# A third SBUF buffer for a unit's q and M in a fused attention and feed-forward kernel

## The chip, the cores and the metric

The kernel runs on one core of one Trainium2 chip. The metric is the device time of one execution in microseconds. The engines are named as the profile names them: PE (matrix products) with PEld (its weight loads), DVE (vector), ACT (scalar), POOL and SP. All transfers of this kernel are issued from SP's queue. Each engine works through its own queue in order, and waits on semaphores of the others.

## The reference, cut

Four sequences of 576 tokens with 8 heads of 64 go through causal attention and a retrieval from a memory matrix M; a gate mixes both, and a feed-forward layer with squared ReLU follows.

```python
scores = scale * np.matmul(q, k.transpose(0, 1, 3, 2))          # causal, softmax -> a
local = np.matmul(a, v)
q_p = np.where(q > 0, q, np.exp(q) - 1.0) + 1.0                  # phi
mem_out = einsum('bhsd,bhde->bhse', q_p, M_prev) / (einsum('bhsd,bhd->bhs', q_p, z_prev)[..., None] + 1e-06)
x = g * mem_out + (1 - g) * local                                # g = sigmoid(beta), per head
out = np.maximum(x @ w_in, 0.0) ** 2 @ w_out                     # 512 -> 2048 -> 512
```

## The kernel before

**Units.** Attention is cut into 24 units, called u0 to u23 here. A unit is one sequence, one pair of heads (their 2 x 64 rows fill the 128 partitions) and a set of query tiles of 128 tokens. The first two sequences have two kinds of units, four with tiles 1 and 2 and then four with tiles 3 and 4; the last two sequences have four units each with all four tiles. (The first 64 tokens of each sequence are done apart at the start.)

**Loads of a unit.** `loads` issues three tiles: `kd` (k, one buffer, `KB = 1`), `qm` (M, z and q, `QB` buffers, line 348; units of tiles 3 and 4 take two transfers, one for M and z and one for q) and `vv` (v, two buffers, `VVB = 2`). They are requested by `after()` in line 464, when the products with M of the unit before have been written down; the first unit's at the start.

**A unit's work.** From u6 on q and k are split into a high and a low part: ACT writes `qh` (line 371), DVE `ql` (372), ACT `kh` (377), POOL or DVE `kl` (378). u0 to u5 use q and k as loaded. ACT takes exp of q (388), and phi is formed, from u6 on in place in `qm` (393, 394), before that in `pe` (399, 400). v is scaled by its largest element (`vx`, `vt`, `vy`) and split into `vs` (425, 427). PE multiplies phi with M (`pm`, line 445, whose PSUM tag `av` has two buffers that it shares with `vt` and `acc`), and that is the last read of a unit's `qm`. Then come the scores (`sp`, line 479, one PSUM buffer), the row minimum and mask on DVE (500), exp on ACT (520), the split of the weights into `a` (558, 560), their transpose by DMA (`aT`, 564), the product with v (`acc`, 585 to 590), and the sum into `memx` (600), which is written to DRAM (611). `qh`, `ql`, `kh` and `kl` have one buffer each.

**Feed-forward.** The tokens are taken in nine blocks. `moe(n)` runs 8 steps: 24 products `up` with the first weight (747 to 749), ReLU and square on ACT (753, 754), a split into `gh` and `gl` (756 to 759), and 12 products with the second weight into `oacc` (737 to 739). In its seventh step it fetches the tokens of the next block (`xn`, 632), transposes them on PE (635, 637) into a PSUM buffer of the tag `up`, and splits them on ACT (640) and DVE (641). The last two blocks run together (`moe_pair`, lines 666 to 721). The weights are loaded and split in stages through about the first 90 us.

**Order.** The program is written down unit by unit; `ORD` merges the first units with the weights and with block 0, the rest of attention follows, and then the other blocks. A planner (`schedule_with_timeline_sim=True`) then fixes, while the program is built, the order of every engine's queue: what is written down first has priority, and what is written later fills the time that is free. So blocks 1 and following run between the attention units. A load into a tile with buffers waits for the last reader of the tile that had the buffer before: with `QB = 2` the `qm` of unit n waits for `pm` of unit n-2.

Of the kernel before, what the change touches and what calls it, by code (L numbers as in the profile page):

```python
# [43 lines left out]
PXT = 'av'  # L44
PXE = 'aa'
PHI = 1
QB = 2
VVB = 2
ZW = D + 1
MW = 576  # L50
# [42 lines left out]
def fused_kernel(ctx: ExitStack, tc: tile.TileContext, t0_d, kk_d, qv_d, beta, w_in, w_out, out):  # L93
# [247 lines left out]
    def loads(b, p, tiles):  # L341
        qa, qb = QT[tiles[0]][0], sum(QT[tiles[-1]])
        kd = at.tile([P, S], F32, tag="kd", name="kd", bufs=KB)
        nc.sync.dma_start(kd[:, :qb], kk_d[b, p, :, :qb])
        qm = at.tile([P, 2 * ZW + SQ], F32, tag="qm", name="qm", bufs=QB)
        qa, qb = qa - D + 2 * ZW, qb - D + 2 * ZW
# [552 lines left out]
```

## Time and profile before

| | us |
|---|---|
| time, median of 3 runs (lowest to highest) | 578.53 (578.21 to 580.98) |
| the profiled execution | 578.71 |
| its span | 576.9 |
| PE busy (share of the span) | 550.8 (95%) |
| PEld busy | 478.6 (83%) |
| DVE busy | 414.0 (72%) |
| ACT busy | 349.6 (61%) |
| POOL busy | 63.7 (11%) |

The span is the time between the first and the last event that the profile shows; 1.8 us of the profiled execution lie outside of it. Busy times of PE and PEld overlap. PEclk is the clock that TensorE was granted, as a share of its full 2.4 GHz. "Waits" rows say which instruction an engine's queue was held at, and what ended the hold.

### The profile page before, as it was taken

To read this page: it belongs to the slowest core of one execution; us is meant where nothing else is said; L and a number is where in the kernel's file an instruction comes from. 1 tells how busy PE (TensorE), PEld (TensorE's weight loads), DVE (VectorE), ACT (ScalarE), POOL (GpSimd) and SP (SyncE) were. 2 spreads that over 40 slices of the span, in tenths; PEclk is the share of its full clock that TensorE was granted. 3 is DMA by queue.
4 is the path that set the end of the run, shared out by engine and by line. 5 is a ranking of instruction groups with operands and counts; after the bars stand their busy time and mean duration, and the time that the engine had idled before them with its cause. 6 is when DMAs were issued, how large, how long until landed. Compare 5 with 4: busy or idle time off the path is not lost.

```text
span 576.9 us, 11597 instructions
## 1 busy us (share of the span) xinstructions
PE 550.8 (95%) x4259; PEld 478.6 (83%) x4259; DVE 414.0 (72%) x1323; ACT 349.6 (61%) x792; POOL 63.7 (11%) x45
## 2 busy tenths in 40 slices
PE   5489998898999999999999999999999999999997
PEld 5378886787888888898988988889889898888885
DVE  6989989897989888989695988969787523212121
ACT  4589976767868767877567675665756222212213
POOL 3749560012010000000000000000000000000000
PEclk9999999799999999999999999999999999999999
DMA  8857654875665466676456736675244610000001
GB/s 310 341 192 286 228 168 111 174 162 136 138 150 159 109 183 151 149 185 168 110 108 124 149 78 163 115 189 143 56 84 83 128 37 1 36 2 0 1 0 73
DMA packets 124856, 74.71 MB, mean 129 GB/s; under 512 B 97152, under 2 KB 110464, under 8 KB 124800
## 3 DMA queue, kind: packets, MB, share of 16 engines
q1 hardware_dynamic: 124800, 73.98, 49.7%
q8 instruction: 33, 0.54, 0.4%
q14 instruction: 23, 0.19, 0.1%
HBM read 41.59 MB, written 8.78 MB: 87 GB/s over the span
## 4 chain that ended last, share of the span: by engine, by line
PE 63%; DVE 12%; ACT 10%; DMA 9%; issue 3%; POOL 1%; SPq 1%; ACTq 0%; DVEq 0%; POOLq 0%
PE oacc L677 8%; PE up L747 6%; PE up L749 6%; PE up L748 6%; PE oacc L737 6%; PE oacc L739 6%; PE oacc L738 6%; PE sp L479 5%; DMA vv<-in_qv_dram 4%; ACT e L520 3%; PE up L692 3%; PE up L691 3%; PE up L693 3%; PE acc L590 2%; PE pm L445 2%
## 5 line engine op out<-in xcount | busy, mean ns | idle before, releaser
L747 PE MATMUL up<-xh,w 128*128 128x256 f32 x448 | 129.5, 289 | 0.0
L748 PE MATMUL up<-xl,w 128*128 128x256 f32 x448 | 128.9, 288 | 0.0
L749 PE MATMUL up<-xh,w 128*128 128x256 f32 x448 | 128.4, 287 | 0.0
L520 ACT ACTIVATE e<-e,mx 128x320 f32<-128x320 f32 (+3 forms) x128 | 77.6, 608 | 50.1 <-DVE memx L600 34.1
L737 PE MATMUL oacc<-w,gh 128*128 128x512 f32 x224 | 89.9, 402 | 0.0
L747 PEld LDWEIGHTS up<-xh,w 128*128 128x128 f32 x448 | 86.0, 192 | 2.9 <-issue 0.6
L738 PE MATMUL oacc<-w,gh 128*128 128x512 f32 x224 | 88.4, 395 | 0.0
L748 PEld LDWEIGHTS up<-xl,w 128*128 128x128 f32 x448 | 86.1, 192 | 2.2
L739 PE MATMUL oacc<-w,gl 128*128 128x512 f32 x224 | 86.4, 397 | 0.4 <-DVE gl L759 0.4
L749 PEld LDWEIGHTS up<-xh,w 128*128 128x128 f32 x448 | 86.1, 192 | 0.7
L560 DVE SCALAR_TENSOR_TENSOR a<-e,a 128x128 f16<-128x128 f32 x116 | 64.1, 566 | 31.1 <-ACT a L558 30.1
L558 ACT ACTIVATE a<-e 128x128 f16<-128x128 f32 x116 | 55.0, 524 | 10.9 <-DMA aT<-a 9.9
L753 ACT ACTIVATE r<-up 128x512 f32<-128x512 f32 x56 | 32.7, 584 | 43.2 <-PE up L749 29.0
L702 DVE CAST gh<-r 128x512 fp32r<-128x512 f32 x15 | 6.4, 427 | 62.4 <-ACT r L701 62.4
L739 PEld LDWEIGHTS oacc<-w,gl 128*128 128x128 f32 x224 | 41.5, 188 | 9.0 <-DVE gl L759 0.9
L738 PEld LDWEIGHTS oacc<-w,gh 128*128 128x128 f32 x224 | 42.3, 189 | 6.6
L500 DVE CUSTOM_DVE_ANT_0 e<-sp,mask 128x320 f32<-128x320 f32 (+3 forms) x128 | 47.0, 417 | 0.9 <-PE sp L479 0.7
L737 PEld LDWEIGHTS oacc<-w,gh 128*128 128x128 f32 x224 | 42.3, 189 | 6.4
L700 ACT ACTIVATE r<-up 128x512 f32<-128x512 f32 x16 | 9.6, 597 | 60.8 <-PE up L693 60.8
L759 DVE TENSOR_TENSOR gl<-r,gh 128x512 fp32r<-128x512 f32 x56 | 38.9, 695 | 2.6 <-ACT gh L756 1.8
L677 PE MATMUL oacc<-w,gh 128*128 128x512 f32 x120 | 36.8, 389 | 0.0
L590 PE MATMUL acc<-vs,aT 128*128 128x128 f16 x302 | 36.7, 220 | 0.0
(153 smaller groups left out, 1160.2 us busy)
## 6 DMA issues: line engine op xcount, KB each, us to landing
raw<-in_w_in_dram SPq DMA_DIRECT2D x11, 512.0 KB, 7.2
vv<-in_qv_dram SPq DMA_DIRECT2D x16, 320.0 KB, 3.3
raw<-in_w_out_dram SPq DMA_DIRECT2D x9, 512.0 KB, 6.6
kd<-in_kk_dram SPq DMA_DIRECT2D x16, 288.0 KB, 3.1
out_dram<-o SPq DMA_DIRECT2D x16, 256.0 KB, 2.1
xd<-memx SPq DMA_DIRECT2D x31, 128.0 KB, 1.9
xn<-xd SPq DMA_DIRECT2D x14, 256.0 KB, 2.9
qm<-in_qv_dram SPq DMA_DIRECT2D x8, 321.0 KB, 2.9
```

The source lines that it names most:

```text
L500: nc.vector.tensor_tensor_reduce(out=e[:, h, ka:kb], in0=sps[:, h, cs], in1=mask[:, 448 - q0 + ka : 448 - q0 + kb], scale=-0.125, scalar=3 ...
L520: ex = nc.scalar.activation(e[:n, h, :ke], e[:n, h, :ke], AF.Exp, bias=bs, scale=-1.0, accum_out=sm[:n, h : h + 1])
L558: nc.scalar.mul(av[:, :, o0 : o0 + w], x, SC)
L560: nc.vector.scalar_tensor_tensor(out=av[:, :, o0 + w : o0 + 2 * w], in0=x, scalar=SC, in1=av[:, :, o0 : o0 + w], op0=ALU.mult, op1=ALU.sub ...
L590: nc.tensor.matmul(o2, aT[:, h * nb + c, :n], vs[:, h, c], start=False, stop=c == i)
L677: mms.append(nc.tensor.matmul(acc[t], g[:, ts], w_out_op(f, part), start=s0, stop=s1))
L737: nc.tensor.matmul(acc[t], gh[:, u, ts], w_out_op(f, 0), start=f == 0, stop=False)
L738: nc.tensor.matmul(acc[t], gh[:, u, ts], w_out_op(f, 1), start=False, stop=False)
L739: nc.tensor.matmul(acc[t], gl[:, u, ts], w_out_op(f, 0), start=False, stop=f == NF - 1)
L747: nc.tensor.matmul(up[:, u, :], w_in_op(f, k, 0), xh[:, k, :], start=k == 0, stop=False)
L748: nc.tensor.matmul(up[:, u, :], w_in_op(f, k, 0), xl[:, k, :], start=False, stop=False)
L749: nc.tensor.matmul(up[:, u, :], w_in_op(f, k, 1), xh[:, k, :], start=False, stop=k == NK - 1)
```

## The change

The pool of the tile `qm` gets three buffers in place of two. One constant is changed, and no instruction is added or removed in the code; a buffer is 642 floats of each partition (2 x 65 for M and z, 512 for q).

```diff
-QB = 2
+QB = 3
 ...
         qm = at.tile([P, 2 * ZW + SQ], F32, tag="qm", name="qm", bufs=QB)
```

With three buffers the load of unit n waits for `pm` of unit n-3.

## Rows read from the trace of the kernel before

**Rows 1.** The page, its first part: busy time, share and instructions by engine.

```profile
PE 550.8 (95%) x4259; PEld 478.6 (83%) x4259; DVE 414.0 (72%) x1323; ACT 349.6 (61%) x792; POOL 63.7 (11%) x45
```

**Rows 2.** Windows: length, PE, PEld, DVE, ACT, POOL busy (instructions), PEclk, DMA share, GB/s.

```profile
17.00:34.00 17.00, 10.19 (x232) 9.49 (x232) 15.14 (x29) 9.90 (x17) 13.20 (x7) 1.00 0.58 230
92.00:110.00 18.00, 14.26 (x82) 10.92 (x82) 16.55 (x63) 8.66 (x19) 0.94 (x2) 0.81 0.84 175
102.00:109.00 7.00, 5.98 (x26) 4.83 (x27) 5.86 (x24) 4.89 (x10) 0.84 (x1) 0.52 0.71 167
110.00:140.00 30.00, 28.86 (x243) 23.84 (x243) 25.76 (x84) 23.55 (x52) 2.97 (x2) 1.00 0.71 165
140.00:170.00 30.00, 28.97 (x250) 25.11 (x248) 25.26 (x93) 21.51 (x59) 3.51 (x3) 1.00 0.63 142
170.00:230.00 60.00, 59.65 (x480) 52.58 (x477) 52.79 (x190) 45.17 (x107) 1.02 (x1) 1.00 0.56 144
230.00:440.00 210.00, 210.00 (x1739) 185.32 (x1738) 173.99 (x603) 140.46 (x325) 0.00 (x0) 1.00 0.59 131
465.00:490.00 25.00, 25.00 (x154) 22.30 (x154) 7.11 (x14) 7.65 (x15) 0.00 (x0) 1.00 0.01 1
```

**Rows 3.** Timeline of PE, 229.7 to 231.3 and 480 to 484: start, duration, line.

```profile
229.80 0.28 PE L747 MATMUL up<-xh,w 128*128 128x256 f32 x1
229.92 0.28 PE L748 MATMUL up<-xl,w 128*128 128x256 f32 x1
...
480.86 0.28 PE L747 MATMUL up<-xh,w 128*128 128x256 f32 x1
480.98 0.28 PE L748 MATMUL up<-xl,w 128*128 128x256 f32 x1
```

**Rows 4.** Waits of SP's queue: total us, times, longest us.

```profile
SPq L351 <- DVE vs L427: 16.6, 14, 3.0
SPq L348 <- PE pm L445: 15.0, 8, 5.0
```

**Rows 5.** The load of qm (line 348): who waited for it, us and times.

```profile
  ACT pe L388: 5.7, 3
  ACT qh L371: 4.2, 4
```

**Rows 6.** Timeline, 238.5 to 250 us: SP's loads and the steps that take them.

```profile
240.27 0.71 PE L445 MATMUL pm<-qm 128*128 128x130 f32 x4
241.02 0.33 SPq L348 DMA_DIRECT2D qm<-in_qv_dram  x1
242.28 0.33 SPq L351 DMA_DIRECT2D vv<-in_qv_dram  x1
244.46 0.61 ACT L371 CAST qh<-qm 128x512 fp32r<-128x512 f32 x1
246.64 0.68 DVE L372 TENSOR_TENSOR ql<-qm,qh 128x512 fp32r<-128x512 f32 x1
248.83 0.42 PE L479 MATMUL sp<-kh,qh 64*128 64x320 f32 x2
```

**Rows 7.** Timeline, 97.7 to 112 us; in brackets the idle time before and what ended it.

```profile
98.05 0.90 SPq L348 DMA_DIRECT2D qm<-in_qv_dram  x2
...
99.53 0.38 SPq L344 DMA_DIRECT2D kd<-in_kk_dram  x1
...
100.36 0.30 PE L637 MATMUL px<-identr,memx 128*128 128x128 f32 x1
...
101.99 0.42 ACT L388 ACTIVATE pe<-qm 128x256 f32<-128x256 f32 x1 [2.81 <-DMA qm<-in_qv_dram]
102.31 0.57 ACT L640 CAST xh<-px 128x512 fp32r<-128x512 f32 x1
...
103.86 2.18 PE L479 MATMUL sp<-kd,qm 64*128 64x448 f32 x8 [1.02 <-DMA kd<-in_kk_dram]
...
106.78 0.41 PE L747 MATMUL up<-xh,w 128*128 128x256 f32 x1
...
106.99 0.41 PE L748 MATMUL up<-xl,w 128*128 128x256 f32 x1
```

## The prediction

> **What bounds the kernel now.** I first read the shares: PE is busy for 95% of the span, DVE for 72% [rows 1]. A share over the whole span hides stages, so the second view is the table of windows [rows 2]. The reader should see three regimes there. Up to 34 us PE is idle much of the time (10.19 of 17.00 us busy from 17 to 34), because the weights and the first tokens are being prepared. From 92 to 230 us PE has small gaps: 18.00 - 14.26 = 3.74 us between 92 and 110, 1.14 to 140, 1.03 to 170 and 0.35 to 230. From 230 to 440 us, where the last nine units or so of attention run between blocks of the feed-forward, PE shows no idle time at all (210.00 of 210.00), nor in the stretch without attention from 465 to 490.
>
> Ends of matmuls are modelled, so a busy PE could hide bubbles. The third view is therefore the distance between starts [rows 3]: 256-column products start 0.12 us apart both beside attention (229.80, 229.92) and alone (480.86, 480.98). Beside attention PE runs at the pace that it has alone, so from 230 us on the time is set by the amount of PE work, and the change takes none away.
>
> The clock is the other thing to see. Between 102 and 109 us the granted clock is 0.52 of full speed, that is nearly all of it at 1.2 GHz [rows 2]; the 256-column products start 0.21 us apart there (106.78, 106.99) [rows 7] in place of 0.12. What PE did before is the gap of 3.74 us. At full clock the 5.98 us of PE work in that stretch would need at least 5.98 x 0.52 = 3.1 us, so the slow clock costs up to 2.9 us. Gap and clock together are 6.6 us, the largest loss after the start.
>
> **What the change removes: the wait of the qm load.** SP's queue stood 15.0 us, in 8 waits, at line 348 until a `pm` product had been done [rows 4]. One case is seen in full [rows 6]: `pm` of u14 starts at 240.27 and takes 0.71; the load of u16 goes out at 241.02, at once; ACT writes `qh` of u16 3.4 us after that (244.46), `ql` comes at 246.64 and the scores at 248.83. So a load that has its buffer one unit earlier would let `qh` come up to 3.4 us sooner in a unit. But that wait stands on the path of attention, not on that of PE: while u16 waits, PE runs products of the feed-forward. What ACT itself lost by waiting for `qm` is 5.7 + 4.2 = 9.9 us in 7 waits [rows 5], on an engine that is busy for 61% [rows 1].
>
> Step by step, by stretches, against the profiled execution of 578.71 us (576.9 span and 1.8 outside):
>
> 0 to 92 us. The load of u2 has a buffer of its own and no wait; it can go out behind the first weight loads, in the stretch from 17 to 34 us, where the DMA engines are busy for 0.58 of the time [rows 2]. Each later load takes the place in SP's queue where the load of the unit before stood, so, if the planner keeps that order, no queue gets longer. I take 0. The bounds are a gain of 0, since the units up to u4 start long after their `qm` has landed (ACT's waits for it number only 7, and the first that I can place is at 101.99), and a loss of 0.9 us, the issue time of two transfers of this kind [rows 7], if they stand ahead of a load that the start waits for.
>
> 92 to 110 us. Here `qm` is on PE's path for once [rows 7]. The load of u5 goes out at 98.05. ACT's queue stands at line 388 for it until 101.99 (2.81 us idle). Behind that instruction is the copy `xh` of block 1's tokens (102.31), though its transpose on PE started at 100.36 and took 0.30. The `up` products of block 0 wait for the PSUM buffer that this copy frees. With three buffers u5 only waits for `pm` of u2, a whole unit earlier, so `xh` can start at about 100.7, 1.6 us sooner. The next to be late is the scores of u5 on PE, which are queued ahead of the `up` products and waited for `kd` until 103.86; `kd` has one buffer and went out at 99.53, behind the two `qm` transfers (0.90 us of SP's time). So the gain is between 0 (if `kd` stays where it is) and 1.6 us, and I take 0.9, what `kd` gains if the two transfers are not ahead of it. The ends for the range are wider: all of 6.6 us, if the gap closes enough that the clock is not lost, and a loss of 0.9, if the loads of u6 stand ahead of `kd` with nothing to show for it.
>
> 110 to 230 us. PE's idle time is 1.14 + 1.03 + 0.35 = 2.52 us in all, and DVE is busy for 25.76 of 30, 25.26 of 30 and 52.79 of 60 us (86%, 84%, 88%) [rows 2]. Earlier `qh` and `ql` can close part of these gaps, none of which is put down to `qm` directly. Bounds: 0 and 2.52; I take 0.6, about a quarter, since the load of `vv`, which waits for `vs` of the unit before last (16.6 us in 14 waits, [rows 4]), stays and becomes the wait that holds SP: in the case of [rows 6] it is 1.26 us behind the `qm` load.
>
> 230 us to the end. 0: no idle time to take [rows 2], the same work, the same pace [rows 3].
>
> The sum is 0.9 + 0.6 = 1.5 us, so 577.2 us against the profiled execution. That execution was 0.18 us above the median of the runs, so I say 577.0 us.
>
> **The rivals.**
>
> The gap closes. Between 92 and 110 us the queues are planned anew, PE gets `up` products or scores in time, and the clock stays at 2.4 GHz. Gain 6.6 us there and about 1 us behind it: 571.1 us. For it speaks that a wait for `qm` is in the chain of this gap; against it that `kd`, the last units' `memx` and DVE (16.55 of 18.00 us busy) are in it too.
>
> PE has hidden room beside attention, and a shorter attention gives it back. Weight loads are busy for 185.32 of 210.00 us, 0.882, from 230 to 440, against 22.30 of 25.00, 0.892, without attention [rows 2]; the difference is 1.1% of 210 us, or 2.3 us, which with the sum above gives 574.9 us. Against it are the equal distances of [rows 3]. [...]
>
> A second gap, on the other side. Because q is there earlier, the planner puts the splits and exponentials of the next unit ahead on ACT and DVE. In the stretch from 110 to 230 us DVE has only 12 to 16% free. Where it gets none, `gl` of the feed-forward comes late, PE runs out of products as it did at 100 us, and the clock falls. The place is a unit's start in that stretch; it decides once DVE is busy for as much as between 92 and 110 us (92%). The price is that of the gap that is there, 3.74 + 2.9 = 6.6 us: 585.1 us by the median, less if part of the sum is gained: 583.6.
>
> Nothing moves. The load is earlier, but `vv` (two buffers) and `kd` (one) take the place of the wait, and PE's gaps are the same: 578.5 us. For it speaks that `vv` follows by 1.26 us in [rows 6].
>
> **How the numbers follow.** The forecast (1 to 2 us saved) gets 0.31, nothing moves 0.14, the gap closes 0.25, hidden room 0.06, a second gap 0.24. The likeliest gives 577.0. A measurement of this kernel can tell about 0.5%, 2.9 us, from no change: faster means below 575.6, slower above 581.4. The first two cases lie within; hidden room and the closed gap lie below; the second gap above, with a few hundredths of it within, where the new gap costs no clock. That makes 0.31 faster, 0.47 the same, 0.22 slower. The range has to take in the closed gap with all of the idle time behind it, 578.5 - 6.6 - 2.5 = 569.4, and the second gap, up to 585.1; leaving the outermost part of both out, it is 570.0 to 584.0. The likeliest case alone would be 574.9 to 578.5.
>
> **What would show it.** Right: the loads of `qm` wait for no `pm`, or hardly, and ACT's 9.9 us of waits for them are gone; SP stands longer at `vv`; PE stays without idle time from 230 us on; the stretch around 100 us keeps a gap of 2 to 4 us and a slow clock. Wrong: a change of more than 1 us behind 230 us, which would mean that PE's amount of work isn't the limit there; a gap around 100 us that is gone, or a new one with a clock of 0.5 elsewhere. The start would be wrong if PE's busy time before 34 us shifts by more than the 0.9 us that I bounded.

## The result and the profile after

| | before | after |
|---|---|---|
| time, median of 8 runs each (lowest to highest), us | 578.86 (576.50 to 581.23) | 582.62 (581.85 to 584.55) |
| ratio, 95% interval | | 1.0051 (1.0027 to 1.0074) |
| the profiled execution, us | 578.71 | 582.10 |
| its span, us | 576.9 | 580.3 |

The third buffer made the kernel about 0.5% slower; the forecast was 577.0 us, 0.26% faster. PE's amount of work did not change. The first part of the page of after answers to [rows 1]:

```profile
PE 550.7 (95%) x4259; PEld 479.7 (83%) x4259; DVE 412.6 (71%) x1323; ACT 349.0 (60%) x792; POOL 62.8 (11%) x45
```

Its windows, with the columns of [rows 2]:

```profile
92.00:110.00 18.00, 13.34 (x75) 10.26 (x75) 16.28 (x62) 8.56 (x18) 1.06 (x2) 0.82 0.73 166
110.00:140.00 30.00, 30.00 (x253) 25.21 (x253) 26.48 (x88) 25.06 (x56) 3.14 (x2) 1.00 0.79 179
140.00:170.00 30.00, 30.00 (x264) 26.46 (x262) 27.45 (x103) 23.38 (x64) 4.18 (x4) 1.00 0.64 148
170.00:230.00 60.00, 59.09 (x470) 52.16 (x469) 52.00 (x183) 44.71 (x104) 0.00 (x0) 1.00 0.63 148
...
290.00:305.00 15.00, 12.57 (x119) 11.38 (x119) 12.21 (x43) 8.39 (x23) 0.00 (x0) 0.89 0.66 117
...
400.00:440.00 40.00, 38.95 (x309) 34.17 (x307) 32.13 (x118) 23.37 (x53) 0.00 (x0) 1.00 0.32 64
```

Against [rows 2], PE's idle time between 110 and 230 us fell from 2.52 to 0.91 us in this execution: a gain of 1.6. Between 92 and 110 us it rose from 3.74 to 4.66. And where PE had no idle time at all, 2.43 us appeared between 290 and 305 us, with a granted clock of 0.89 of full speed, and 1.05 us between 400 and 440. Those two new gaps are more than the gain. They are there too in a second profiled execution of the same program (e8 below: 2.26 and 1.03 us); the slow clock beside the first is not (1.00 there).

What PE waited for near 298 us is in the timeline of SP, PE and ACT (start, duration, line; in brackets the idle time before and what ended it).

```profile
291.71 6.11 SPq L564 DMA_TRANSPOSE aT<-a  x2
...
297.35 0.45 PE L635 MATMUL px<-identr,xn 128*128 128x128 f32 x4
300.23 0.23 PE L585 MATMUL acc<-vs,aT 128*128 128x128 f16 x1 [2.43 <-DMA aT<-a]
...
300.27 0.83 ACT L558 ACTIVATE a<-e 128x128 f16<-128x128 f32 x2 [1.47 <-DMA aT<-a]
301.01 0.57 ACT L640 CAST xh<-px 128x512 fp32r<-128x512 f32 x1
```

The waits of after (total us, times, longest us):

```profile
SPq L351 <- DVE vs L427: 27.0, 14, 4.5
SPq L348 <- PE pm L445: 22.0, 9, 5.3
...
ACT a L558 <- DMA aT<-a: 18.2, 16, 2.6
PE acc L585 <- DMA aT<-a: 3.5, 2, 2.4
PE sp L479 <- DMA kd<-in_kk_dram: 2.9, 1, 2.9
ACT qh L371 <- DMA qm<-in_qv_dram: 1.9, 1, 1.9
```

The view of line 564 of after tells how long its transposes took from issue to landing; in the kernel before that line reads 2.5/3.9/5.7.

```profile
DMA to landing us min/median/max: 2.8/4.1/6.2
```

The transposes of the weights `a` by DMA (line 564) came late. PE's queue stood at the product `acc` that needs one; ACT stood at the copy into `a` whose buffer the transpose was to free, and `xh` of the feed-forward's tokens was queued behind it, so PE could not fill the gap with `up` either. The loads of `qm`, on which the change was argued, are no longer an issue for ACT (1.9 us here and 1.4 at line 388, against 9.9 in [rows 5]). But they still wait for `pm` on SP, longer than in [rows 4] (22.0 us against 15.0).

### The profile page after: what moved, and what is told of

The parts are those of the page before. It is cut to its first block, busy times and chain, and to the rows that moved or that the text cites. A ratio compares the mean times of both kernels' runs of the same rounds, so it can differ in the third digit from the quotient of the medians.

```text
span 580.3 us, 11585 instructions
## 1 busy us (share of the span) xinstructions
PE 550.7 (95%) x4259; PEld 479.7 (83%) x4259; DVE 412.6 (71%) x1323; ACT 349.0 (60%) x792; POOL 62.8 (11%) x45
## 4 chain that ended last, share of the span: by engine, by line
PE 77%; DVE 9%; DMA 7%; POOL 3%; issue 3%; ACT 1%; SPq 1%; DVEq 0%; POOLq 0%; ACTq 0%
PE up L747 8%; PE up L748 8%; PE up L749 8%; PE oacc L677 8%; PE oacc L737 7%; PE oacc L739 7%; PE oacc L738 7%; PE sp L479 7%; PE acc L590 3%; PE up L693 3%; PE up L692 3%; PE pm L445 3%; PE up L691 2%; DMA aT<-a 2%; POOL raw L180 2%
```

## The experiments

All were timed against the kernel before on the same chip; ratios are to it, with 95% intervals. Executions of the kernel before itself spread between 576.4 and 584.8 us in these batches, so one of them alone says little below 1%.

### The order or the waits?

The planner makes a new order of all queues for three buffers. Four runs took order and waits apart. **e1_old_order** keeps every queue in the order of the plan for two buffers and has three; only the waits of the `qm` loads differ.

```diff
+    nc, arrays = build(2, None)          # QB = 2: its queues give the order
+    nc, arrays = build(3, queues(nc))    # QB = 3 in that order
+    for n, m in zip(seq, seq[1:]):
+        tc.add_manual_dep(ins[m], n, AFTER, reason="order of the other plan")
```

> Three buffers, but every engine's queue keeps the order that the planner made for two buffers; only the waits of the qm loads for pm are gone. Theory A (the loss comes from the new order of the queues, and PE did not wait for qm): PE's idle time from 92 us on stays within 1 us of that of the kernel before, no gap near 300 us, 577 to 579 us. Theory B (the earlier loads themselves disturb the transposes or other transfers): transposes land later than the 3.9 us median of before, and the time is 581 to 584 us, as after.

**e2_swap** is the changed kernel with two transposes of the gap at 298 us exchanged on SP, so that the one that PE waits for is issued first.

```diff
+    seq.remove("I-3278")
+    seq.insert(seq.index("I-3317"), "I-3278")
```

> The changed kernel with the order of its queues kept, but for one pair: the two transposes that SP issued at 291.7 and 294.5 us change places, so that the one for which PE stood until 300.2 us goes first. Theory A' (the loss is this one gap, an order of two transposes): the gap of 2.4 us and its slow clock go, the time falls by 2 to 4 us to 579 to 580. Theory B (three buffers cost in general, and the gap only shows where): the gap moves, 582 to 583 us.

**e3_two_written** (two buffers) and **e4_three_written** (three) hold the transposes in the order in which they are written down and let the planner place the rest.

```diff
-                nc.sync.dma_start_transpose(out=aT[:, :, :n], in_=a[:n])
+                turn(tc, nc.sync.dma_start_transpose(out=aT[:, :, :n], in_=a[:n]))   # behind the last one
```

> A control with two buffers: the planner is only told to keep the transposes in the order in which they are written down, which gives new orders on PE, DVE, ACT and SP. Theory A (what the change moved is mainly the luck of a new plan): the time differs from before by 1 to 4 us, in a direction that I can't foresee, 575 to 583 us, with gaps of PE at other places. Theory B (a plan's details matter little, three buffers cost): 578.3 to 579.5 us.

> Three buffers with a third plan: the transposes are kept in the order in which they are written down. Theory A: no loss that belongs to three buffers, 576 to 581 us, and the gap near 298 us is gone, since its two transposes were out of the written order. Theory B: 582 to 584 us as after.

| | median, us | ratio |
|---|---|---|
| e1_old_order | 586.95 | 1.0100 (1.0072 to 1.0129) |
| e2_swap | 581.91 | 1.0025 (1.0001 to 1.0049) |
| e3_two_written | 580.82 | 0.9988 (0.9963 to 1.0013) |
| e4_three_written | 579.09 | 0.9962 (0.9937 to 0.9987) |

e1 was the surprise. With the queues of the kernel before and waits only taken away, it should have been no slower than 577 to 579 us; it was slower than the changed kernel. So the new order of the queues could not be the whole cause, and something else had come with the third buffer. e2 has a smaller gap (13.55 of 15.00 us busy from 290 to 305 us, against 12.57), but its gain on the changed kernel can't be told from none. e3 shows that the written order of the transposes alone is worth nothing that can be told; with three buffers (e4) the kernel is 0.4% faster than before.

### The early loads or the place of the tiles?

Two things were left in e1: the `qm` loads go out earlier, and the third buffer (642 floats, which take 2592 bytes as allocated) moves every tile that lies behind `qm` in SBUF. **e5_same_waits** keeps the order and gives the loads back the waits that they have with two buffers, so only the places differ. **e6_first_free** frees the loads of u2 to u7 alone, **e7_last_free** those of u8 to u23; **e8_after_again** is the changed kernel, held to its own order in the way in which e5 to e7 are held to the old one.

```diff
+    for load, readers in TIED.items():   # e5: all units, e6: u8 to u23, e7: u2 to u7
+        for n in readers:                # what the load waits for with two buffers
+            tc.add_manual_dep(ins[load], n, DependencyInfo(DependencyClass.Sync, DependencyReason.DATA), ...)
```

> Three buffers, but every queue in the order of the plan for two buffers, and every load of qm waits for the same instructions as with two buffers (pm of the unit before last). Against the kernel before, only the places of tiles in SBUF differ. Theory C (it is the early loads that cost: the transfers that now go out earlier meet the transposes and stores and delay these): ratio 0.9975 to 1.0025. Theory D (the place of the tiles costs, not the waits): 1.007 to 1.013, as with the old order and free loads.

> As the run before in this batch, but the loads of u2 to u7 are free to go one unit earlier (they wait for pm of the third unit before, or nothing). Theory C: the old order with free loads was 1.6 us behind the kernel before at 112 us and 3.3 us at 165 us of the span, so 1.003 to 1.006. Theory D: 1.007 to 1.013.

> The complement: the loads of u8 to u23 are free, those of u2 to u7 wait as with two buffers. Theory C: the old order with free loads lost another 5 us behind 200 us, so 1.004 to 1.008. Theory D: 1.007 to 1.013. If C is right the two parts together give the 1.0% of the old order with free loads.

> The changed kernel itself (three buffers, its own order, its own waits), on this chip, as the measure for the other three. Both theories: 1.003 to 1.007, as in its own comparison. A ratio of 1.000 or below would mean that its loss belongs to single executions and not to the order.

| | median, us | ratio |
|---|---|---|
| e5_same_waits | 587.16 | 1.0081 (1.0048 to 1.0114) |
| e6_first_free | 588.72 | 1.0119 (1.0082 to 1.0157) |
| e7_last_free | 586.20 | 1.0083 (1.0054 to 1.0112) |
| e8_after_again | 583.41 | 1.0040 (1.0013 to 1.0067) |

Theory C falls, theory D stands: with the same instructions, the same order and the same waits, the kernel is 0.8% slower once its tiles lie elsewhere, and which loads are free makes no difference that can be told. The way of holding an order costs nothing that can be told either: e8 is as slow as the changed kernel itself (1.0040 and 1.0051).

### Which places?

The kernel before has nearly all tiles on a grid of 64 bytes, and a third buffer moves them 32 bytes off it (2592 = 40 x 64 + 32). **e9_same_waits_aligned** is e5 with the tile of k 32 bytes larger, which restores that grid. **e10_two_shifted** is the kernel before, two buffers, with that same enlargement, which breaks it. **e11_after_aligned** and **e12_three_written_aligned** put the changed kernel and e4 on the grid by a wider `qm`.

```diff
-        kd = at.tile([P, S], F32, tag="kd", name="kd", bufs=KB)
+        kd = at.tile([P, S + 8], F32, tag="kd", name="kd", bufs=KB)                 # e9, e10
...
-        qm = at.tile([P, 2 * ZW + SQ], F32, tag="qm", name="qm", bufs=QB)
+        qm = at.tile([P, 2 * ZW + SQ + 14], F32, tag="qm", name="qm", bufs=QB)      # e11, e12
```

> The run with three buffers in the old order and with the old waits, but the tile of k is 32 bytes larger, so that every tile behind qm begins at a multiple of 64 bytes of its partition again (the third buffer had moved them all by 2592 bytes, 32 more than a multiple of 64). Theory D1 (a begin off the 64-byte grid costs): 0.9975 to 1.0025. Theory D2 (another effect of the place, or of the third buffer, whatever the grid): 1.005 to 1.011, as without the 32 bytes.

> The kernel before with two buffers and nothing else changed than the tile of k, 32 bytes larger: all tiles behind it begin 32 bytes off the 64-byte grid. Order and waits are those of the kernel before. Theory D1: 1.005 to 1.011, without any third buffer; transposes land at 4.1 us in the median in place of 3.9. Theory D2: 0.9975 to 1.0025.

> The changed kernel with the tile of qm 14 floats wider, so that its buffers are 2624 bytes apart and all tiles begin on the 64-byte grid; order and waits are those of the changed kernel. Theory D1: it gives back the 0.8% of the place, from 1.004 to 0.994 to 0.999, which is what the prediction said of the waits. Theory D2: 1.001 to 1.007.

> Three buffers, transposes in the written order (0.9962 before), and the tile of qm 14 floats wider as in the run before. Theory D1: another 0.4 to 0.8% faster, 0.988 to 0.993. Theory D2: 0.994 to 0.999.

| | median, us | ratio |
|---|---|---|
| e9_same_waits_aligned | 586.42 | 1.0109 (1.0078 to 1.0141) |
| e10_two_shifted | 586.48 | 1.0100 (1.0070 to 1.0130) |
| e11_after_aligned | 582.70 | 1.0043 (1.0020 to 1.0066) |
| e12_three_written_aligned | 579.64 | 0.9986 (0.9963 to 1.0008) |

Neither theory fits: e9, e11 and e12 came out as D2 has it, e10 as D1. The 64-byte grid is not it, and yet the place counts: e10 has 32 bytes more in one tile, two buffers, nothing else, and 1.0% is gone. Its windows show where.

```profile
110.00:140.00 30.00, 28.47 (x240) 23.54 (x240) 26.55 (x85) 23.51 (x51) 2.97 (x2) 1.00 0.78 177
140.00:170.00 30.00, 28.57 (x244) 24.91 (x244) 24.82 (x90) 21.20 (x56) 3.53 (x3) 1.00 0.60 132
170.00:230.00 60.00, 58.51 (x459) 51.40 (x459) 51.59 (x186) 44.48 (x104) 1.02 (x1) 1.00 0.59 141
350.00:400.00 50.00, 48.95 (x391) 42.74 (x389) 39.14 (x136) 30.95 (x73) 0.00 (x0) 1.00 0.64 136
400.00:440.00 40.00, 38.36 (x336) 33.96 (x335) 34.06 (x118) 22.82 (x55) 0.00 (x0) 1.00 0.44 93
```

The view of line 564 of e10, from issue to landing:

```profile
DMA to landing us min/median/max: 2.8/4.2/6.6
```

PE idles 4.45 us between 110 and 230 us (2.52 in [rows 2]), and 1.05 and 1.64 us where it had not idled at all. The transposes land later, and not only on average: the fastest takes 2.8 us in place of 2.5. The rest of e10's trace shows no such slowing where it was compared: PE, DVE and ACT are busy for 551.3, 414.8 and 351.0 us (550.8, 414.0 and 349.6 in [rows 1]), and the median packet of other transfers takes what it took (27 ns for 512 bytes, 102 ns for 2560 bytes, in both). The durations of single packets in the trace say it more sharply. The transposes move 92160 packets of 256 bytes. Here is how many of those took more than 18 ns, the median, and the times that 90 and 95 in 100 stay within:

```
                    a begins at    over 18 ns   median  90%  95%   (ns)
before              multiple of 512     2.4%      18     18   18
after               512 n + 32         21.0%      18     31   42
e5_same_waits       512 n + 32         19.8%      18     29   42
e9_..._aligned      512 n + 64         19.6%      18     29   42
e10_two_shifted     512 n + 32         18.6%      18     28   41
e11_after_aligned   512 n + 128        19.9%      18     29   42
```

The mean over all packets would be a poor measure (22.1 ns before, 22.6 after): in each of these runs fewer than 0.5% of them take over 200 ns, and these alone add 1 to 4 ns to it. In the kernel before, `a`, from which the transposes read, begins at a multiple of 512 bytes of its partition. That gave the next theory: what counts is the larger grid.

**e13_two_512** moves all tiles behind k in the kernel before by 512 bytes. **e14_old_order_512**, **e15_after_512** and **e16_three_written_512** are e1, the changed kernel and e4 with the tile of k 480 bytes larger, so that everything behind `qm` is moved by 2592 + 480 = 3072 = 6 x 512 bytes.

```diff
-        kd = at.tile([P, S], F32, tag="kd", name="kd", bufs=KB)
+        kd = at.tile([P, S + 128], F32, tag="kd", name="kd", bufs=KB)     # e13
+        kd = at.tile([P, S + 120], F32, tag="kd", name="kd", bufs=KB)     # e14, e15, e16
```

> The kernel before, two buffers, with the tile of k 512 bytes larger: all tiles behind it are moved, but keep their place on a grid of 512 bytes (a, the source of the transposes, begins at a multiple of 512 bytes, as before). Theory D3 (it is the place on the 512-byte grid that counts, through the 256-byte packets of the transposes, of which 95 in 100 took 18 ns in the kernel before and the slowest tenth 28 to 32 ns in every kernel with other places): 0.9975 to 1.0025, and transposes land in 2.5 us at least and 3.9 in the median. Theory D4 (any move of the tiles costs this order of the queues 1%, as 32 bytes did): 1.007 to 1.013.

> Three buffers, the order of the plan for two, free loads of qm (1.010 before), and the tile of k 480 bytes larger, so that all tiles behind qm are moved by 3072 bytes, a multiple of 512, against the kernel before. What is left of the change is the wait alone. Theory D3: 0.995 to 1.001; 0.997 is what the prediction's sum gives. Theory D4: 1.007 to 1.013.

> The changed kernel, its own order and waits, with the tile of k 480 bytes larger, so that a begins at a multiple of 512 bytes again. Theory D3: the transposes land as in the kernel before and the gap at 298 us shrinks: 0.992 to 1.000. Theory D4: 1.002 to 1.007, as it was and as it was on the 64-byte grid.

> Three buffers, transposes in the written order (0.9962 and, on the 64-byte grid, 0.9986), and the tile of k 480 bytes larger. Theory D3: 0.987 to 0.995. Theory D4: 0.994 to 1.001.

| | median, us | ratio | packets over 18 ns |
|---|---|---|---|
| e13_two_512 | 580.98 | 1.0004 (0.9980 to 1.0028) | 2.3% |
| e14_old_order_512 | 581.65 | 1.0010 (0.9984 to 1.0036) | 2.5% |
| e15_after_512 | 578.32 | 0.9953 (0.9931 to 0.9975) | 1.7% |
| e16_three_written_512 | 576.34 | 0.9913 (0.9881 to 0.9945) | 2.1% |

Theory D3 holds in all four. Moving the tiles costs nothing when they stay on the 512-byte grid (e13). On that grid the changed kernel, with its own order and waits, is 0.5% faster than before instead of 0.5% slower: the place of the tiles had cost it 1.0051 - 0.9953 = 0.0098, some 5.7 us (5.0 us with the 1.0040 of e8). With the transposes in the written order it is less, 0.9962 - 0.9913 = 0.0049 or 2.8 us (e4 against e16): what the place costs may depend on the order. The gap near 298 us in the timeline of e15:

```profile
289.40 3.81 SPq L564 DMA_TRANSPOSE aT<-a  x2
...
296.73 0.23 PE L585 MATMUL acc<-vs,aT 128*128 128x128 f16 x1 [0.82 <-DMA aT<-a]
```

The landing of its transposes:

```profile
DMA to landing us min/median/max: 2.5/3.6/6.2
```

The same two transposes keep SP's queue for 3.81 us in place of 6.11 (5.83 in e8, 5.55 in e11, both with that order off the grid), and PE waits 0.82 us in place of 2.43. The windows of e15:

```profile
92.00:110.00 18.00, 13.55 (x86) 10.77 (x85) 16.16 (x63) 9.61 (x21) 1.49 (x2) 0.91 0.78 167
110.00:140.00 30.00, 29.78 (x266) 24.93 (x265) 27.54 (x90) 24.91 (x56) 3.81 (x3) 1.00 0.72 180
140.00:170.00 30.00, 30.00 (x251) 26.48 (x249) 27.49 (x103) 23.94 (x65) 3.32 (x3) 1.00 0.65 152
170.00:230.00 60.00, 60.00 (x491) 52.98 (x490) 53.61 (x189) 45.96 (x104) 0.00 (x0) 1.00 0.60 152
290.00:305.00 15.00, 14.18 (x130) 12.57 (x128) 13.14 (x52) 10.41 (x27) 0.00 (x0) 1.00 0.67 124
```

e14 answers the question that e1 had been made for: with the places put right, the freed waits alone, in the old order, are worth nothing that can be told (1.0010). Its windows between 110 and 230 us leave 2.48 us idle, as before:

```profile
110.00:140.00 30.00, 29.22 (x247) 24.14 (x245) 25.92 (x84) 23.93 (x52) 2.97 (x2) 1.00 0.70 169
140.00:170.00 30.00, 28.72 (x248) 24.94 (x246) 24.77 (x91) 21.11 (x56) 3.52 (x3) 1.00 0.62 139
170.00:230.00 60.00, 59.58 (x477) 52.51 (x476) 52.57 (x190) 45.05 (x106) 1.02 (x1) 1.00 0.56 141
```

No load of `qm` waits for `pm` any more in e14; SP simply stands at `vv` instead, as its waits show:

```profile
SPq L351 <- DVE vs L427: 29.9, 14, 6.3
```

The loads of `qm` stand in the same queue as those of `vv`, and ACT still waits 9.1 us for `qm` in e14 (4.7 at line 388 and 4.4 at line 371), against 9.9 in [rows 5]. So what e15 gains, it gains with the new order of the queues; that the same order would gain nothing with two buffers was not run. e16 is the fastest kernel of the study: three buffers, transposes in the written order, tiles on the grid.

### Source or target?

A transpose reads `a` and writes `aT`. **e17_source_moved** and **e18_target_moved** take the kernel before. The first moves the buffer of `a` from which 42 of the 58 transposes read, with `vs` and `s3`, by 64 bytes; the second moves what lies ahead of them, with the buffer of `aT` into which those 42 write.

```diff
-            vz = at.tile([P, 2], F32, tag="vz", name="vz", bufs=2)
+            vz = at.tile([P, 16], F32, tag="vz", name="vz", bufs=2)[:, :2]      # e17: 64 bytes ahead of vs and a
+            vz = at.tile([P, 64], F32, tag="vz", name="vz", bufs=2)[:, :2]      # e18: with 64 bytes more in kd, 512
...
-                s3 = at.tile([P, 2, D], F32, tag="s3", name="s3", bufs=1)
+                s3 = at.tile([P, 2 * D + 112], F32, ...)[:, : 2 * D]...          # e17: 512 for what lies behind
```

> The kernel before, two buffers, its order and waits. Only vs, s3 and the buffer of a from which 42 of the 58 transposes read are moved by 64 bytes off the 512-byte grid; the tiles ahead stay, those behind are moved by 512 bytes. Theory S (it is where the source of a transpose begins): 1.005 to 1.011, and the slowest tenth of the 256-byte packets takes 25 to 32 ns in place of 18. Theory T (it is the target, or any other tile): 0.998 to 1.003, packets at 18 ns.

> The complement: the kernel before with all tiles from qm to vz, among them vv and the buffer of aT into which 42 of the 58 transposes write, moved by 64 bytes, while vs, a and all behind them keep their place on the 512-byte grid (moved by 512 bytes). Theory S: 0.998 to 1.003, packets at 18 ns. Theory T: 1.005 to 1.011, the slowest tenth of the packets at 25 ns or more.

| | median, us | ratio | packets over 18 ns | 90% | 95% |
|---|---|---|---|---|---|
| e17_source_moved | 581.48 | 1.0011 (0.9993 to 1.0028) | 10.9% | 20 ns | 29 ns |
| e18_target_moved | 581.50 | 1.0019 (1.0001 to 1.0038) | 2.4% | 18 ns | 18 ns |

The packets follow the source. The 42 transposes hold 432 of the 720 blocks of 128 x 128 (the other 16 have 2 x 9 blocks each), 60%; were all packets of moved sources slow as often as in e10, the share would be 2.4 + 0.6 x (18.6 - 2.4) = 12%, and it is 10.9%. The target changes nothing in them, and e18's time of 1.0019 lies where no effect was expected (0.998 to 1.003). The fastest transpose of e17 lands in 2.8 us, that of e18 in 2.5. The landing line of e17:

```profile
DMA to landing us min/median/max: 2.8/4.0/5.4
```

The time, however, does not follow: e17 was to lose 0.5 to 1.1% and loses 0.1%. That the 42 smaller transposes are slower is mostly hidden. Where e10 and e17 differ is in the sixteen large ones, whose buffer of `a` keeps its place on the grid in e17. The kernels in this table keep the same order on SP's queue, so the same transposes can be set side by side (medians of the trace's records, us):

| | large, 16 of 58: on SP's queue | large: landing | small, 42 of 58: landing | all 58: on SP's queue, sum |
|---|---|---|---|---|
| before | 2.0 | 4.1 | 3.5 | 100.6 |
| e13_two_512 | 2.0 | 4.1 | 3.5 | 99.9 |
| e18_target_moved | 2.1 | 4.0 | 3.5 | 99.1 |
| e17_source_moved | 2.0 | 4.1 | 4.0 | 99.2 |
| e10_two_shifted | 2.8 | 4.7 | 4.0 | 114.5 |
| e5_same_waits | 2.7 | 4.6 | 3.9 | 111.1 |

A small transpose with a moved source lands some 0.5 us later and holds SP's queue hardly longer; a large one holds that queue for 0.7 to 0.8 us more, and all 58 together for 10 to 14 us more. The kernels that lose 0.8 to 1.0% are those with this longer queue. That it is the large ones, or the large and the small ones together, that carry the 1% of e10 is therefore likely, but no run moved the buffer of the large ones alone, and it is not shown.

## Why the prediction went wrong

**What bounds the kernel.** PE does, and its busy time is the same (550.7 us after, 550.8 in [rows 1]); the time is told by PE's idle time and clock. That part held.

**The step that failed: "no queue gets longer", and a sum in which one more buffer is nothing but one wait less.** The working counted what the change removes (waits) and what it moves (loads). The prediction writes that sentence of the first 92 us and on the condition that the planner keeps its order; the stretches behind take it for granted, up to the 0 "230 us to the end". But the planner did not keep its order, and SP's queue did get longer: the 58 transposes held it for 111.2 us after, 100.6 before and 94.1 in e15 (the new order on the grid). The working did not count that a third buffer moves nearly every other tile by 2592 bytes, and no term and no rival of the prediction stands for that. That is the missing term: 5.0 to 5.7 us with the new order (e15 against the changed kernel), 4.7 to 5.8 us with the old one (0.81 to 1.00% of 580 us, e5 and e10). It stands in no diff and in no wait on `qm`, where the prediction looked; the profile of after shows it in the landing of the transposes, 2.8/4.1/6.2 us against 2.5/3.9/5.7, and in the new waits for `aT`. What makes the packets slow is not shown. Those of 256 bytes were slow when their source began 32, 64 or 128 bytes off a multiple of 512 (18.6 to 21.0% of them took over 18 ns), and not at multiples of 512 (1.7 to 2.5%). Why only about a fifth take longer there, while the median stays at 18 ns, is open. Whether a multiple of 256 would do was not tried.

**The step "230 us to the end: 0".** It was argued from there being no idle time to take. That bounds the gain and says nothing of a loss; a stretch in which PE is busy throughout can still be starved. After the change 3.49 us of idle time appeared there (2.43 of them near 298 us), and the clock was 0.89 between 290 and 305 us. The gaps came again in e8 (3.29 us in all), the slow clock did not. With the tiles on the grid (e15) it is 0.82 us, at full clock.

**92 to 110 us: 0.9 taken, lost 0.9.** The first link came as foreseen: `xh` starts at 100.87, 1.44 us earlier than in [rows 7]. The rest is the wide bound of the prediction, loads of u6 ahead of `kd` with nothing to show for it. The timeline of after:

```profile
98.65 0.90 SPq L348 DMA_DIRECT2D qm<-in_qv_dram  x2
99.64 0.38 SPq L344 DMA_DIRECT2D kd<-in_kk_dram  x1
...
100.87 0.59 ACT L640 CAST xh<-px 128x512 fp32r<-128x512 f32 x1
...
103.64 2.19 PE L479 MATMUL sp<-kd,qm 64*128 64x448 f32 x8 [2.86 <-DMA kd<-in_kk_dram]
105.76 1.23 PE L445 MATMUL pm<-qm,pe 128*128 128x130 f32 x4
106.64 0.56 PE L747 MATMUL up<-xh,w 128*128 128x256 f32 x1
```

In the kernel before, `pm` ran ahead of the scores, inside the gap:

```profile
101.90 0.94 PE L445 MATMUL pm<-qm,pe 128*128 128x130 f32 x4 [1.24 <-DVE s L592]
```

`kd` goes out at 99.64 (99.53 before) and the scores start at 103.64 (103.86). The new order puts `pm` behind the scores and ahead of `up`, so that the first `up` starts at 106.64 (105.97 before). The gap stays in e15 too (4.45 us idle), so its size does not hang on the places of the tiles. That the new order widened it by 0.9 is less sure: with the queues of the kernel before it is 3.84 us in e14, 4.02 in e13 and 4.42 in e18. Of the 2.4 and 1.2 GHz that the working names, the trace of before shows a rate: from 465 to 490 us, at a granted clock of 1.00, products of 512 and of 256 columns start 227 and 120 ns apart (medians), so 256 columns more take 107 ns, 2.4 columns per ns; from 103 to 109 us, at 0.50, products of 256 columns start 213 ns apart, 1.2 columns per ns.

**110 to 230 us: 0.6 taken.** One execution of after gained 1.6 us here; but e8, the same program, idles 1.85 us, and the kernel before idles 1.56 us when all its tiles are moved by 512 bytes (e13), so the gain of after can't be told from the spread of single executions. Only e15 is clear of it (0.22 us idle, 2.3 less than in [rows 2]). The reason was not the foreseen one: with free loads in the old order nothing was gained (e14, 2.48 us idle). It takes the new order of the queues.

**The signs that it named.** ACT's waits for `qm` fell from 9.9 to 3.3 us and SP stands longer at `vv` (27.0 us, 16.6 in [rows 4]): right in the main. "PE stays without idle time from 230 us on": wrong, 3.49 us. "The loads of `qm` wait for no `pm`, or hardly": wrong, 22.0 us in 9 waits. The new order puts the loads further ahead (the last one goes out at 361.6 us, 392.3 before), and they then wait for `pm` of the third unit before as they had for that of the second. In the old order (e14) there are none, and nothing is gained by it. The start was within its bound: 16.9 us idle up to 92 us against 16.2, where 0.9 was allowed. (In this execution of after the clock was 0.75 up to 34 us; in e8, the same program, it was 1.00 there.)

**The rivals.** A second gap came, in one of two executions with a slow clock beside it, and the time lies between no change and its two prices. Its place and its mechanism did not: it stood near 298 us and not before 230, and PE waited for transposes, not for `gl`. That a gap brings the slow clock was the author's estimate from the one at 100 us; in e18 PE idles 4.42 us between 92 and 110 us at a clock of 1.00. The gap near 100 us did not close, and hidden room gave nothing: attention's last store went out at 449.39 us, 9.7 us before that of the kernel before, and the time did not fall. No run shows that the busy share of weight loads, from which the 2.3 us of that rival are worked out, tells of room on PE; after, products of 256 columns start 120 ns apart beside attention (median, 230 to 440 us) and alone (465 to 490), as before. "Nothing moves" is what the waits alone do (e14).

**What is left of the forecast.** Without the missing term the change is worth 0.47% (e15, 0.25 to 0.69%), 2.7 us, where 1.5 were forecast. That the two are near is luck as far as the argument goes: the waits that were to give it gave nothing by themselves (e14), and the stretch from 92 us, which was to give most of it, has no less idle time in e15 than before.

## What to carry to other kernels

Adding a buffer moves every tile that is allocated behind it, and a DMA transpose notices where its source begins (here 18.6 to 21.0% of its packets took over 18 ns off the 512-byte grid, 1.7 to 2.5% on it): before a plan or a wait is blamed, keep the order and the waits and change only the places, and try the tiles, the sources of transposes above all, on the grid that they had (here 480 bytes of padding turned 0.5% slower into 0.5% faster, and with the transposes in the written order 0.4% faster into 0.9%). A stretch without idle time bounds what can be gained there at zero, not what can be lost (here 3.49 us of idle time came from 230 us on). A wait that is taken away gives nothing by itself when another load ahead in the same queue goes on waiting (here `vv`, 29.9 us in e14, with a ratio of 1.0010); ask what the planner can do with it.

## What the runs showed of the hardware

- A transpose by DMA from SBUF to SBUF depends on where its source lies in the partition: with sources 32, 64 or 128 bytes off a multiple of 512, 18 to 21% of its 256-byte packets took over 18 ns (95% stayed within 41 or 42), against 1.7 to 2.5% on the grid (95% within 18); the median stayed at 18 ns. The target, moved by 64 bytes, did not matter for the 42 transposes whose target was moved.
- A transpose of 18 blocks of 128 x 128 held SP's queue for 2.7 to 2.8 us in the median with its source off the grid (e10, e5) and for 2.0 to 2.1 us on it (before, e13, e17, e18). The smaller ones landed about 0.5 us later (e17, e10, e5) and held the queue hardly longer.
- 32 bytes of padding ahead of the tiles, with the same instructions, order and waits, made this kernel 1.0% slower; 512 bytes made it 0.04% slower, which is no difference.
- Two transposes kept SP's queue for 5.55 to 6.11 us off the grid (after, e8, e11) and for 3.81 us on it (e15), at the same place of the same order.
